# A table of some 3,500 steps, made anew: attention and a GELU MLP on one core

## The chip, the cores and the metric

One core of a Trainium2 chip runs the whole program. The metric is device time in microseconds (us), the median of several executions; smaller is better. TensorE (PE) multiplies matrices, VectorE (DVE), ScalarE (ACT) and GpSimd (POOL) work on tiles in SBUF and PSUM, and SyncE (SP) issues every DMA of this kernel. Each engine runs its own instructions strictly in the order in which the program gives them, and waits for the others through semaphores.

## What is computed

```python
scores = (q @ k^T) / sqrt(64)                 # 8 batches x 8 heads, 576 positions, 64 wide
scores = where(0 <= i-j < 128, scores - slope_h*|i-j|, -1e9)
x = softmax(scores) @ v                       # then as 4608 tokens x 512
h = x @ w_in                                  # 512 -> 2048
out = gelu(h) @ w_out                         # 2048 -> 512
```

All inputs and the output are fp32.

## The kernel before

**Tiles.** The 4,608 tokens are nine tiles of 512; a batch has 576 tokens, so batch b fills the end of tile b and the beginning of tile b+1. While the MLP of tile t runs, the attention of batch t+1 is made. A batch has four units, one for each pair of heads.

**Accuracy.** A factor is split into an fp16 high part and an fp16 low part, and a product is three fp16 products added in PSUM. So each operand that another engine makes costs a high part (a scaled copy) and a low part (a subtraction, mostly on DVE).

**One unit of attention** goes through these steps, named by a letter, the unit k and for M and N the half r of the unit's columns:

- S: scores on PE (L640). B: scale and bias from PSUM to SBUF on DVE (L666), with a memset on POOL (L672).
- M: softmax. A maximum on DVE (L749), exponentials on ACT (L753), the sums inverted on DVE (L756, L757), the weights scaled on POOL (L763, a piece of 128x192 each), the high part by a cast on ACT (L765).
- N: the low part of the weights, a subtraction on DVE (L772), and then a DMA on SP that transposes both parts into `et` (L776). A unit has two such halves, N{k}0 and N{k}1.
- Y: weights times v on PE (L821). It can start when the transposes have landed. X: the result as high and low part of x (ACT L841, DVE L323).

**One tile of the MLP.** In tiles 1 and 2 h is made by L868 (step H) and GELU follows (g). From tile 3 on h is made in blocks by sums of sub-blocks (steps 1 to 7, L1080 on PE; a, c, d, e with L1122 and L323 on DVE, L1131 on POOL), for which step Z makes sums of x first: `Z0` on POOL, `Z1` on DVE (L1004 to L1013). The second matrix is step o (L913; L910 in tile 0; one step of a tile is 12 matmuls). Tiles 7 and 8 have sub-block sums in the second product as well (L1230). The statistics of the next batch's v and q are the steps v and q: an absolute maximum over v (L391, DVE), then short operations that bring it over the partitions (L293 to L304, DVE), then powers of two and scales (L313 to L318, L522, L563).

**The order.** No scheduler decides it. Every step is a Python generator, and a long string names which one goes on next; the order of the steps is the order of the instructions on each engine. Two more strings tell which PSUM bank and which output buffer each allocation takes, in that order.

```python
    with tc.manual_schedule(engines=None):
        for step in ORDER.split():
            next(later[step])
```

In `ORDER`, a step's first digit is the tile in whose time it stands and the rest is as above: `3N31` is the second half of the low weights of unit 3 in the time of tile 3 (batch 4). A leading `0` before another digit is such a step that the tasks of the first tiles hold (`02y3`: batch 2, unit 3).

Of the kernel before, what the change touches and what calls it, by code (L numbers as in the profile page):

```python
# [68 lines left out]
0H2 0j6 0j5 0j3 0H5 0H5 0lv 0H0 0p2 0H1 0j4 0L2 0L3 0H5 0a6 0p2 0i4 0lv 0j5 0j5 0lv 0i4 0H4 0H5 0H8 0H9 0H9 0H9 0a7  # L69
0a7 0j3 0j3 0i5 0i5 0H8 0H8 0g1 0H11 0H11 0g4 0j7 0H9 0a6 0H11 0g3 0j6 0j6 0H10 0p3 0i3 0i3 0f 0p3 0A0 0p3 0p3 0p3  # L70
0H10 0H10 0j7 0j7 0g2 0H6 0H6 0lv 0v1 0i6 0H6 0i6 0g0 0H8 0i7 0H6 0H10 0i7 0p2 0f 0f 0A1 0p3 0J0 0H11 0A0 0A2 0J0 0J0
0lq 0lq 0f 0J2 0g11 0H7 0H7 0H7 0g5 0A2 0v1 0v1 0v1 0v1 0v1 0g9 0H15 0H15 0H15 0H15 0H7 0g7 01c 0v1 0v1 01c 0A1 0g8
0J2 0H12 0J2 0J1 0J1 0J1 0f 0u1 0q1 0q1 0u1 0q1 0q1 0H12 0q1 0q1 0q1 0A3 0J3 0A3 0J3 0J3 0H14 0H14 0H13 0H13 0H14 0H14
0H12 0H13 0O 0O 0q1 0d 0q1 0q1 0q1 0g6 0O 0O 0O 0H13 0g13 0g14 0O 0O 0d 0f 0A4 0f 0H12 0g15 0A4 0S1 0B1 0B1 0B1 0B1
0S0 0B0 0A5 0O 0B0 0B0 0g10 0S0 0S0 0B0 0B0 0B0 0S1 0S1 0B0 0B0 0B0 0g12 0M00 0o 0o 0J4 0J4 0J4 0M00 0B1 0B1 0J6 0o 0o
0o 0o 0A6 0J5 0M01 0M01 0M01 0M01 0M01 0S2 0M00 0A6 0M00 0J6 0J6 0f 0M01 0M01 0lV 0M10 0M00 0S2 0M00 0o 0o 0M01 0O
0M00 0M00 0M00 0A5 0M00 0M00 0M00 0M00 0N00 0N00 0N01 0N00 0N00 0N00 0A7 0M01 0lV 0M01 0M01 0J7 0B1 0lV 0B1 0N01 0N01
# [36 lines left out]
2H13 2H13 2M11 2g15 2g15 2g15 2B2 2M21 2M11 2M11 2o1 K K K K 2H14 2H13 2H13 2g13 2g13 2g14 2g14 2g13 K K 2M20 2g14 K
# [1348 lines left out]
```

## Time and profile before

| | us |
|---|---|
| median of 3 runs | 874.3 (873.79 to 874.45) |
| profiled execution | 870.3 |
| its span | 868.2, granted clock 0.998 |
| PE busy | 840.5 (97%) |
| DVE busy | 719.7 (83%) |
| ACT busy | 618.6 (71%) |
| POOL busy | 322.3 (37%) |

The profile was taken in one execution, 4.0 us below the median of the runs. A timeline row gives the start, the length, the engine, the line, the operation with the tiles it writes and reads, the number of instructions run together into the row, and in brackets how long the engine had stood idle before it and what released it. A view by windows gives each engine's busy time in a stretch and the granted TensorE clock there.

### The profile page before, as it was taken

Reading aid. Unit: us, or ns where it says so; the run is one execution under the profiler, and the core shown is the slowest. Engines: PE = TensorE matmul, PEld = TensorE weight load, DVE = VectorE, ACT = ScalarE, POOL = GpSimd, SP = SyncE. Lnnn points to the kernel's source line nnn. Section 1 sums busy time; section 2 is a strip of 40 time slices with the busy share of each in tenths; the row PEclk is TensorE's granted clock in tenths of the full one; section 3 lists DMA queues with packets and bytes.
Section 4 is the critical chain, followed back from the end, with each engine's and each line's share of the span. In section 5 each row is a group of like instructions: output and inputs, shape, how many; then the busy total and the mean of one; then the engine's idle time right before and its main releaser. Section 6 shows DMA issues by size and latency. Waiting matters only on the chain.

```text
span 868.2 us, 19703 instructions
## 1 busy us (share of the span) xinstructions
PE 840.5 (97%) x7860; PEld 548.4 (63%) x7860; DVE 719.7 (83%) x1278; ACT 618.6 (71%) x1246; POOL 322.3 (37%) x509
## 2 busy tenths in 40 slices
PE   6999999999999999999989998999999999999998
PEld 4654444544554455884568555865587467888887
DVE  6999999999899976988996989789868856774763
ACT  7999898887778867766758776765776646654661
POOL 2010100242027674577614973477526762000000
PEclk9999999999999999999999999999999999999999
DMA  9755485534553457474754685447651673341301
GB/s 314 272 165 200 157 246 148 145 108 112 111 140 123 107 172 208 139 160 137 166 155 157 143 206 176 141 86 194 177 196 16 182 181 146 121 159 31 117 1 49
DMA packets 180939, 129.45 MB, mean 149 GB/s; under 512 B 134384, under 2 KB 157040, under 8 KB 177136
## 3 DMA queue, kind: packets, MB, share of 16 engines
q1 hardware_dynamic: 180848, 128.21, 51.2%
q8 instruction: 61, 1.00, 0.5%
q14 instruction: 30, 0.25, 0.1%
HBM read 75.89 MB, written 17.83 MB: 108 GB/s over the span
## 4 chain that ended last, share of the span: by engine, by line
PE 47%; DVE 12%; POOL 4%; ACT 4%; DMA 3%; issue 2%; SPq 0%; DVEq 0%; POOLq 0%; ACTq 0%
PE u L1080 14%; PE v L1080 10%; PE o L913 7%; PE h L868 5%; PE u_out L1230 4%; POOL s L763 2%; DVE s L666 2%; PE sc L640 2%; DMA k<-kp 2%; PE av L821 1%; DMA et<-e_main 1%; DVE e_main L772 1%; PE z_out L1230 1%; PE x_out L1230 1%; PE v_out L1230 1%
## 5 line engine op out<-in xcount | busy, mean ns | idle before, releaser
L913 PEld LDWEIGHTS <-g 128*128 128x128 f16 x1152 | 111.1, 98 | 131.9 <-POOL g L891 0.6
L913 PE MATMUL o<-wo,g 128*128 128x512 f16 x864 | 191.8, 379 | 0.0
L753 ACT ACTIVATE s<-s,nmax 128x192 f32<-128x192 f32 x252 | 111.4, 443 | 32.3 <-DVE nmax L749 31.8
L868 PE MATMUL h<-x,wi 128*128 128x512 f16 x576 | 128.1, 379 | 0.3 <-DVE wi L323 0.2
L763 POOL TENSOR_SCALAR s<-s,z 128x192 f32<-128x192 f32 x180 | 103.1, 588 | 33.4 <-DVE z L757 20.0
L1080 PEld LDWEIGHTS <-t 128*128 128x128 f16 x1008 | 98.3, 98 | 12.2 <-DMA t<-stored 0.3
L868 PEld LDWEIGHTS <-wi 128*128 128x128 f16 x576 | 55.3, 98 | 68.9 <-issue 2.3
L1080 PEld LDWEIGHTS <-wi 128*128 128x128 f16 x864 | 84.3, 98 | 13.2 <-issue 1.4
L666 DVE SCALAR_TENSOR_TENSOR s<-sc,cs,bias_h 128x384 f32<-128x384 f32 x112 | 65.0, 605 | 1.9 <-PE sc L640 1.0
L913 PE MATMUL o<-wo_first,g 128*128 128x512 f16 x288 | 66.0, 379 | 0.1
L672 POOL MEMSET s<- 64x64 f32 (+1 forms) x112 | 19.2, 172 | 116.5 <-DVE s L666 103.3
L749 DVE TENSOR_REDUCE nmax<-s 128x5 f32<-128x960 f32 (+1 forms) x56 | 58.0, 1042 | 3.6 <-POOL s L672 2.6
L1080 PE MATMUL u<-xs,t 128*128 128x256 f16 x504 | 60.3, 273 | 0.0
L772 DVE TENSOR_TENSOR e_main<-s,e_main 128x768 f16<-128x768 f32 (+1 forms) x40 | 47.6, 1196 | 12.7 <-ACT e_main L765 12.7
L910 PE MATMUL o<-zo,g 128*128 128x512 f32 x128 | 56.9, 597 | 0.0
L640 PE MATMUL sc<-kbuf,qbuf 64*64 64x192 f16 (+3 forms) x1656 | 48.9, 251 | 7.6 <-ACT qbuf L541 4.4
L821 PE MATMUL av<-et,vbuf 128*64 128x64 f16 (+2 forms) x1392 | 43.4, 221 | 10.7 <-DMA et<-e_main 9.0
L1131 POOL TENSOR_SCALAR g<-rooms,sg 128x512 f16<-128x512 f32 x48 | 39.1, 820 | 36.5 <-issue 19.2
L821 PEld LDWEIGHTS <-vbuf 128*64 128x64 f16 x1392 | 40.7, 112 | 18.4 <-issue 14.8
L765 ACT CAST e_main<-s 128x768 f16<-128x768 f32 (+1 forms) x40 | 35.9, 905 | 21.7 <-POOL s L763 15.0
L323 DVE SCALAR_TENSOR_TENSOR g<-rooms,sg,g 128x512 f16<-128x512 f32 x48 | 41.8, 885 | 7.1 <-POOL g L1131 7.1
L753 ACT ACTIVATION_READ_ACCUMULATOR s<-s,nmax 128x1 f32 x252 | 47.3, 188 | 0.0
(253 smaller groups left out, 1697.2 us busy)
## 6 DMA issues: line engine op xcount, KB each, us to landing
t<-stored SPq DMA_DIRECT2D x21, 1024.0 KB, 5.2
v<-vp SPq DMA_DIRECT2D x32, 320.0 KB, 4.6
out<-ob SPq DMA_DIRECT2D x34, 256.0 KB, 2.7
raw<-w_in SPq DMA_DIRECT2D x8, 1024.0 KB, 10.8
raw<-w_out SPq DMA_DIRECT2D x8, 1024.0 KB, 6.3
q<-qp SPq DMA_DIRECT2D x7, 1152.0 KB, 5.7
k<-kp SPq DMA_DIRECT2D x7, 1152.0 KB, 7.0
stored<-sums SPq DMA_DIRECT2D x8, 512.0 KB, 2.6
```

The source lines that it names most:

```text
L640: done = nc.tensor.matmul(ps[bank][o, n, gap:W], a, m[:, gap:W], start=(i == 0 and (n == 0 or b > 0)), stop=(i == len(terms) - 1 and b > 0 ...
L666: yield nc.vector.scalar_tensor_tensor(out=s[:, bank[0] : bank[0] + k, :], in0=ps[bank][:, 0:k, 0:W], scalar=cs, in1=bias.broadcast_to([P, ...
L749: yield nc.vector.tensor_reduce(out=nmax[:, r], in_=s[:, r], axis=AX.X, op=ALU.max, negate=True)
L753: yield nc.scalar.activation(s[:, i, :], s[:, i, :], AF.Exp, bias=nmax[:, i : i + 1], accum_out=z[:, i : i + 1])
L763: yield nc.gpsimd.tensor_scalar(to, s[:, i], z[:, i : i + 1], 1.0, op0=ALU.mult, op1=ALU.mult)
L772: yield nc.vector.tensor_tensor(out=e[:, r, 1, c], in0=st.s[:, r], in1=e[:, r, 0, c], op=ALU.subtract)
L821: done = nc.tensor.matmul(av[r, (js[0] - blocks[0]) * QB : (js[-1] + 1 - blocks[0]) * QB], v32s[b][:, hp, kb, r] if b < EXACT else vbuf[:, ...
L868: done = nc.tensor.matmul(ph, wi[n][:, a, cc, k * P : (k + 1) * P], x[:, cc, b, :], start=(i == 0), stop=(i == 3 * NCC - 1),)
L910: done = nc.tensor.matmul(o, g[:, r, c], zo[n][:, n % 2, k * DM : (k + 1) * DM], start=(fc == first), stop=(fc == last))
L913: done = nc.tensor.matmul(o, g[:, r, a, c], wo[n][:, b, k, :], start=(fc == first and i == 0), stop=(fc == last and i == 2),)
L1080: done = nc.tensor.matmul(ps[:, k * HT : (k + 1) * HT], w(a, i)[:, k * P : (k + 1) * P], m(b, i), start=first and n == 0, stop=True, skip_ ...
L1230: done = nc.tensor.matmul(self.ps[name][:, tb], f(d, a)[:, k, tb * P : (tb + 1) * P], w(d, b, k), start=first, stop=True, skip_group_check ...
```

## The change

The string `ORDER` is another one from its tenth line on (the first 255 of its 3,534 steps, about 54 us, are the same), and with it `PSUM_BANKS` and `ROOMS`. The steps are the same ones, each as often as before; every engine has the same instructions with the same operands' sizes. The table is one line shorter, so every line of code behind it has a number lower by one after the change (L763 is L762). The line of the table in which the scores of unit 3 stand in the time of tile 3, and two lines of the other strings:

```diff
-3M20 3M20 L 3M20 3M20 3M11 3M21 3S3 3N11 3N11 3M21 3M21 3M21 3o1 3o1 3M20 3M20 3Q 3B3 3B3 3B3 3B3 3B3 3q 3M21 3v 3M21
+3M11 3o0 3M11 411 3B2 3B2 3B2 L 3c3 3o0 3B2 3e3 3M11 3v L L L 3M20 3k0 3k0 3o2 3N10 3M20 3S3 3N10 3v 3v 3v 3B2 3M21 L
...
-    "0123456701234567012345760215761340213402135017624762426734015327160725072450372450245450245061450741"
+    "0123456701234567012345760215761340213402135017624762426701325674250671307641307130713130713052106401"
...
-    "20120120202102102012102121201021212102102102120210210120210121210121120221021010120202120120"
+    "20121202002201210220210212120122220102101201201022102012012021012010210121021020202012012012"
```

On PE the scores of unit 3 in the time of tile 3 (`3S3`) stand 12 matmuls of the second matrix (one step o) earlier: between them and the first matmul of `3Y3` there were 96 of those and now there are 108, and that first matmul of `3Y3` is the same PE instruction, counted from the program's start, in both.

**POOL, in the time of tile 3, between unit 3's scores and `3Y3`** (`s_3` are the weights of unit 3, `xr_0` the sums of step Z0 for tile 4). Before:

```order
L1131 TENSOR_SCALAR g_3_4907<-m_3_2_4917,sg_0_3432 128x2x256
L763 TENSOR_SCALAR s_3_5377<-s_3_5377,z_3_5391 128x192 x9
L1004 TENSOR_TENSOR xr_0_5698<-x_4192 128x1024
L1006 TENSOR_TENSOR xr_0_5698<-xr_0_5698 128x256
L1007 TENSOR_TENSOR xr_0_5698<-xr_0_5698 128x256
```

Now:

```order
L1130 TENSOR_SCALAR g_3_4875<-m_3_2_4920,sg_0_2687 128x2x256
L762 TENSOR_SCALAR s_3_5387<-s_3_5387,z_3_5435 128x192 x5
L1003 TENSOR_TENSOR xr_0_5610<-x_4150 128x1024
L1005 TENSOR_TENSOR xr_0_5610<-xr_0_5610 128x256
L762 TENSOR_SCALAR s_3_5387<-s_3_5387,z_3_5435 128x192 x4
L1006 TENSOR_TENSOR xr_0_5610<-xr_0_5610 128x256
```

Two sums of step Z0 now stand ahead of the last four pieces of the unit's weights.

**DVE, in the time of tile 5, the second weights of unit 1** (`s6_1`; `stv7` is the statistic of the last batch's v). Before:

```order
L772 TENSOR_TENSOR e_main_95<-s6_1_7769,e_main_95 128x5x192
L756 TENSOR_SCALAR z6_2_8003<-z6_2_8003 128x5
L522 TENSOR_SCALAR cx6_6_8013<-pwv6_6525,sx6_6820 128x1
L772 TENSOR_TENSOR e_main_95<-s6_1_7769,e_main_95 128x4x192
L757 RECIPROCAL z6_2_8003<-z6_2_8003 128x5
L749 TENSOR_REDUCE nmax6_2_7934<-s6_2_7894 128x4
L391 TENSOR_REDUCE stv7_8040<-v32_7_7675 128x1
L293 COPY quarters_8118<-stv7_8040 32x1
```

Now:

```order
L390 TENSOR_REDUCE stv7_7991<-v32_7_7676 128x1
L986 TENSOR_TENSOR wsums2_0_7825<-wsums2_0_7825 128x1024
L755 TENSOR_SCALAR z6_1_7947<-z6_1_7947 128x4
L756 RECIPROCAL z6_1_7947<-z6_1_7947 128x4
L292 COPY quarters_8067<-stv7_7991 32x1 x2
L322 SCALAR_TENSOR_TENSOR g5_3_7661<-rooms5_2_7618,sg5_0_6068,g5_3_7661 128x2x256
L771 TENSOR_TENSOR e_main_95<-s6_1_7759,e_main_95 128x5x192
```

The maximum over v stood behind the unit's two halves of second weights and now stands ahead of both; the other half's L771 follows seven rows later, with the next steps of the statistic (two more L292, L293, L295) between.

## Rows read from the trace of the kernel before

**Rows 1.** By windows: PE, PEld, DVE, ACT, POOL busy, granted clock, DMA share, GB/s.

```profile
54.00:300.00 246.00, 243.06 (x1847) 118.27 (x1845) 233.42 (x447) 207.75 (x413) 63.62 (x102) 1.00 0.52 151
383.70:432.50 48.80, 48.80 (x460) 26.47 (x453) 44.66 (x91) 31.36 (x76) 35.56 (x61) 1.00 0.61 147
470.00:525.00 55.00, 55.00 (x560) 32.74 (x558) 50.31 (x101) 39.89 (x94) 41.43 (x69) 1.00 0.64 157
438.01:442.00 3.99, 3.99 (x51) 3.37 (x52) 3.31 (x6) 1.94 (x3) 0.25 (x1) 0.59 0.81 236
520.00:540.00 20.00, 16.87 (x243) 10.45 (x242) 17.97 (x34) 12.21 (x13) 7.13 (x7) 1.00 0.55 158
```

**Rows 2.** Timeline of PE: rows that PE came to after a wait.

```profile
152.46 1.58 PE L821 MATMUL av<-et,vbuf 128*64 128x256 f16 x54 [1.30 <-DMA et<-e_main]
...
244.83 2.34 PE L821 MATMUL av<-et,vbuf 128*64 128x256 f16 x72 [0.68 <-DMA et<-e_main]
...
353.08 2.78 PE L1080 MATMUL v<-x,wi 128*128 128x256 f16 x24 [0.68 <-DVE s L666]
...
438.01 2.17 PE L821 MATMUL av<-et,vbuf 128*64 128x256 f16 x42 [3.31 <-DMA et<-e_main]
...
532.28 1.59 PE L821 MATMUL av<-et,vbuf 128*64 128x128 f16 x60 [3.13 <-DMA et<-e_main]
...
596.40 2.72 PE L821 MATMUL av<-et,vbuf 128*64 128x128 f16 x78 [0.79 <-DVE s L666]
...
623.29 1.54 PE L821 MATMUL av<-et,vbuf 128*64 128x128 f16 x42 [0.58 <-DMA et<-e_main]
...
720.23 0.71 PE L1080 MATMUL u<-xs,qbuf 128*128 128x256 f16 x5 [1.43 <-ACT room_s L1187]
```

**Rows 3.** Timeline of DVE: rows at which DVE waited for PE.

```profile
383.70 0.69 DVE L1122 TENSOR_TENSOR m<-v,m 128x512 f32<-128x512 f32 x1 [0.85 <-PE v L1080]
...
459.66 0.69 DVE L1122 TENSOR_TENSOR rooms<-v,rooms 128x512 f32<-128x512 f32 x1 [2.91 <-PE v L1080]
```

**Rows 4.** DVE, operations that the change moves, and the weights' low parts.

```profile
420.86 0.20 DVE L302 STREAM_TRANSPOSE back<-spread 32x32 f32<-32x32 f32 x1
...
428.58 0.55 DVE L323 SCALAR_TENSOR_TENSOR x<-av,cx,x 128x320 f16<-128x320 f32 x1
...
429.46 3.09 DVE L772 TENSOR_TENSOR e_main<-s,e_main 128x960 f16<-128x960 f32 x2
...
592.84 2.80 DVE L391 TENSOR_REDUCE stv<-v 128x1 f32<-128x2560 f32 x1
```

**Rows 5.** SP and the whole run: transposes of the weights, issue, and landing after it.

```profile
410.93 2.06 SPq L776 DMA_TRANSPOSE et<-e_main  x1
...
592.02 1.61 SPq L776 DMA_TRANSPOSE et<-e_main  x1
...
DMA to landing us min/median/max: 3.6/4.1/8.4
```

**Rows 6.** PE: weights times v of units 0 and 1, in tile 3's time.

```profile
414.71 2.88 PE L821 MATMUL av<-et,vbuf 128*64 128x256 f16 x84
```

**Rows 7.** DVE and POOL at 713 us: sums of step Z beside each other.

```profile
713.27 0.42 DVE L1006 TENSOR_TENSOR xr<-xr 128x256 f32<-128x256 f32 x1
713.72 2.30 DVE L1007 TENSOR_TENSOR xr<-xr 128x256 f32<-128x256 f32 x1
...
713.62 2.12 POOL L1013 TENSOR_TENSOR xs<-xr,xs 128x1024 f16<-128x1024 f32 x1 [4.21 <-ACT xs L1012]
```

**Rows 8.** POOL: the last weights of unit 3 in tile 3, and step Z0.

```profile
423.20 2.43 POOL L763 TENSOR_SCALAR s<-s,z 128x192 f32<-128x192 f32 x6 [1.60 <-DVE z L757]
425.60 2.12 POOL L1004 TENSOR_TENSOR xr<-x 128x1024 f32<-128x1024 f16 x1
427.80 0.72 POOL L1006 TENSOR_TENSOR xr<-xr 128x256 f32<-128x256 f32 x1
```

**Rows 9.** The page's groups: count, busy us, mean ns, idle before and releaser: the cast.

```profile
L765 ACT CAST e_main<-s 128x768 f16<-128x768 f32 (+1 forms) x40 | 35.9, 905 | 21.7 <-POOL s L763 15.0
```

More of the change, by code (lines that the diff above doesn't have):

```diff
@@ L73 @@
[L73 to L77, printed above, removed]
@@ new lines @@
+0O 0g12 0q1 0q1 0q1 0q1 0A3 0J3 0q1 0g11 0H7 0A3 0J3 0J3 0f 0q1 0q1 0O 0O 0g7 0O 0lV 0q1 0A4 0J4 0S1 0A4 0B1 0S0 0B0
+0H14 0S0 0S0 0B1 0B1 0g14 0B0 0o 0lV 0B0 0B0 0B0 0B0 0A5 0B0 0B0 0J5 0M00 0M00 0M00 0o 0J4 0B0 0M01 0J6 0S1 0S1 0M00
+0o 0o 0J4 0f 0o 0A6 0B1 0B1 0B1 0B1 0M00 0M00 0M10 0A6 0S2 0M01 0M01 0S2 0o 0o 0o 0o 0B1 0o 0M01 0M01 0M00 0J6 0M00
+0M00 0M00 0M00 0lV 0M00 0M00 0B1 0M11 0M11 0M11 0M01 0N00 0N00 0J6 0N00 0N00 0N00 0M10 0M01 0M01 0M01 0M01 0A5 0N01
+0N01 0N01 0M10 0N00 0M01 0N01 0B2 0N01 0M10 0B2 0B2 0B2 0B2 0M20 0S3 0M10 0M10 0M10 0M11 0S2 0M11 0M11 0M10 0M10 0M10
@@ new lines @@
+0O 0J5 0J5 0O 0O 0M20 0M20 0O 0O 0A7 0B2 0M10 0M10 0B2 0M20 0M20 0M20 0B2 0lQ 0B2 0M21 0M11 0M11 0N10 0N10 0N10 0M20
+0lQ 0N11 0M11 0N11 0M10 0S3 0N10 0M21 0M11 0M11 0N10 0N11 0N11 0B3 0B3 0A7 0B3 0zs 0B3 0M21 0M21 0M21 0J7 0tl 0J7 0J7
+0M21 0zs 01c 0S3 0N11 0v2 0B3 0B3 0q2 0q2 0zs 0o 0O 0O 0O 0v2 0v2 0v2 0v2 0v2 0zs 0v2 0zs 0zs 0zs 0M21 0M21 0M21 0M21
+0o 0M21 0o 0Y0 0B3 0B3 0M30 0N10 0M20 0M20 0M20 0v2 0M30 0M20 0M20 0B3 0y0 0zs 0M20 0q2 0q2 0Y1 0M31 0M30 0M30 0M31
+0zs 0k3 0q2 0M30 0N21 0v1 0N21 0q2 0q2 0v2 0v2 0N20 0N20 0q2 0N20 0N20 0N20 0v2 0y1 0x1 0q2 0v2 0v2 0k2 0v2 0v2 0q2
@@ new lines @@
+03q 03q 0h2 0h2 01g1 02B1 02B1 01H2 01g1 01g4 02B1 01g2 01g2 01H10 01H10 01H10 02B1 0h2 01s 02S1 02S0 02B0 0h3 01H8
+01H8 01H6 02B0 02B0 01g2 01g1 01H10 01g10 02B0 01g10 02B1 02B1 02B1 01H5 02u 01H5 02M00 01H5 01H5 01g5 01H9 01H9 01H9
+01H14 01H14 01H14 01H6 01H6 02B1 01H14 01H12 01H12 02M01 01H12 01g5 02M10 01g5 0h3 02M00 02M00 02B1 02M11 0h3 0h3
+01H12 0h3 01g10 01H13 01g0 02u 03v 03v 0v2 02M01 02M01 02M01 02M01 01H13 01H13 01H15 02M00 02M00 02M00 02M00 01g12
+01H13 01g12 01H8 02M01 02M01 02M01 01H15 02M00 02M00 02M00 01g7 01g7 02M00 01H6 03Q 01g12 03Q 01H15 01H15 01o3 03v
@@ new lines @@
+2o3 2o3 2Y2 2X1 2Y2 2o3 2N30 2M31 2M31 2N31 2N31 2Y3 2Y3 3T1 2q 2q 2q 2q 2X2 2q 2q 2q 2q 2q 2q 2q 2q 2q 2Z0 2Z0 2q 2q
+2o3 2q 2q 2X2 310 2X0 2q 2q 2k2 2q 2q 2q 2Z0 2Z0 2Z0 2X3 2X3 2k3 2X2 2X2 3gs 2Z0 312 3S0 2X3 2X3 2Z1 3B0 2Z1 2Z1 2Z1
+3a0 311 321 3a1 3T0 3a2 3B0 3B0 3B0 2Z1 2Z1 3U 4gs 320 3B0 3B0 2Z1 323 3M00 3M00 3M00 361 3c1 3a1 3a0 3U 3M00 3M00
+3M00 360 3c0 3B0 2k2 3a0 3B0 3B0 371 3a1 350 370 3d0 3M00 3M00 3M00 3M00 3M00 3d1 3a1 3M00 3a1 351 3d1 3M00 3M00 3d0
+3d0 3d0 313 3a3 340 3e0 3a0 341 3N00 3e0 3M01 3a3 3T2 3d1 3d0 330 3e1 3e1 3e1 3d1 3M01 3M01 322 2k3 3T3 362 3c0 3e0
@@ L195 @@
+    "7364102357102365470236452364531264023615023615762035760215764207641203162403612703612407513407651234"
+    "70623470364512065432016541405716245037624056240752630460235412765024132673401536"
 )
 ROOMS = (
-    "20120120202102102012102121201021212102102102120210210120210121210121120221021010120202120120"
+    "20121202002201210220210212120122220102101201201022102012012021012010210121021020202012012012"
 )
```

216 lines of the change are left out of this document (99 added, 117 removed).

## The prediction

> **What bounds the kernel now.** The table shows PE busy for 840.5 of 868.2 us. The change gives PE the same instructions, so it can only move the 27.7 us in which PE stood idle, and the few in which its clock was low. Part of that idle time lies in the first 54 us, which do not change, and behind the last matmul, where both tables end with the same steps. So I read PE's waits first [rows 2]: between 54 and 865 us the longest have one cause. In five of these eight rows the product of weights and v waits for the transposed weights. The two longest, 3.31 and 3.13 us, belong to unit 3 in the time of tiles 3 and 4. Then the windows [rows 1]: behind the 3.31 us wait the granted clock was 0.59 for 3.99 us, that is a mean between the two levels, 1.2 and 2.4 GHz; behind the 3.13 us wait it stayed at 1.00. So the first wait cost 3.99 x 0.41 = 1.6 us more than itself.
>
> Next, who makes the weights late. DVE was busy for 233.4 of 246.0 us from 54 to 300 us, 44.7 of 48.8 us before the 3.31 us wait and 50.3 of 55.0 us before the other [rows 1]. It runs through its list almost without a gap there, and then, at 459.66, waits 2.91 us for PE [rows 3]. So in each tile DVE falls behind PE by the end of the attention and catches up in the middle products. Within such a stretch the delay of PE at a product with v is: where the weights' last operation stands on DVE's list, against where the product stands on PE's. **That is the measure I price the change by**: for each product, how many DVE operations came ahead of its weights, less how much PE work came ahead of it. A wait that stands earlier in the same stretch is not added to a later one; the later only takes what is missing.
>
> **The change, stretch by stretch.** *54 to 360 us.* At 152.46 the weights move ahead by 1.0 us on DVE and the product back by some matmuls, so the 1.30 us wait [rows 2] goes. The operations that made room stand a little later: 3.4 us more of short DVE operations now come before batch 2's unit 1, and the product of unit 0 and 1 there may wait up to 2 us. What PE gains or loses in this stretch it meets again at 353.08, where the first middle product waited 0.68 us [rows 2] for the end of DVE's work on unit 0 of the next batch; DVE's list up to there is the same within 0.5 us. I take **-0.2**; the ends are -2.7 (1.30 + 0.68 + 0.68, all these waits gone) and +1.5.
>
> *Tile 3.* PE reaches both products at the same place of its list as before. Ahead of unit 1's second weights there are now eight short operations of the statistic of v and the scales, 0.2 us or less each [rows 4], together 1.4 us. The transpose was issued at 410.93 and lands 4.1 us later by the median [rows 5], 415.0; unit 1's product is the second half of the row at 414.71 [rows 6], whose two units alternate, and needs it at 415.2. So there is 0.2 us to spare, and a new wait of 1.2 us. For unit 3, one low part of x of 0.55 us and one short operation went behind the weights [rows 4], three short ones ahead: 0.5 us earlier. The total delay at the product of unit 3 then is 3.3 - 0.5 = 2.8 us, of which 1.2 is already waited out at unit 1 and 1.6 stands at unit 3: **-0.5**. The earlier scores (the 108 matmuls instead of 96) do not add to this, because DVE's list and not the scores set the end; if they do, it is a gain, the third rival below. And no wait in this stretch is as long as 3.13 us, after which the clock stayed up: the fall goes, **-1.6**; the ends are -1.6 and 0.
>
> *The two sums of Z0 on POOL, now ahead of unit 3's last four pieces.* Before, POOL was through at 425.60 [rows 8], a cast takes 0.9 us [rows 9], and DVE took up the last low part only at about 429.46 + 1.55 = 431.0 [rows 4]: 4.5 us to spare. The sums cost 2.12 + 0.72 = 2.8 us [rows 8]. So they hide behind DVE's list, and I cost them at **0**; that cover is what the slower rival takes away.
>
> *Tile 4.* PE's places are again the same. A low part of x more (0.55), a short operation less ahead of unit 3's weights: **+0.4** on 3.13. Unit 1's weights come 1.3 us later, and what that makes PE wait is taken off the wait at unit 3.
>
> *Tile 5.* The maximum over v, 2.80 us [rows 4], and six short operations, some 0.9 together, now come ahead of unit 1's second weights: 3.7 us. The transpose was issued at 592.02 [rows 5] and lands at 596.1; the product is the last 42 of the 78 matmuls from 596.40 on [rows 2], that is from 597.7 on: 1.6 us to spare, so a new wait of 2.1 us. The 0.79 us wait at 596.40 stays. At 623.29 the 0.58 us wait goes: the product stands 2.7 us later on PE's list, its weights 0.6 us later on DVE's. 0.79 + 2.1 against 0.79 + 0.58: **+1.5**; the ends are 0 and +2.3 (no spare time beyond the issue's own length).
>
> *Into tile 7.* The first product with sums of x waited 1.43 us [rows 2]; 12 more middle matmuls, 0.116 us each by the row at 353.08 [rows 2], now stand between: **-1.4**. Two POOL sums of weights that ran beside DVE's sums of x here come earlier as well, which only makes this surer.
>
> Sum: -0.2 - 0.5 - 1.6 + 0.4 + 1.5 - 1.4 = **-1.8 us**. The profiled execution was 870.3 us, 4.0 below the median; 870.3 becomes 868.5, and the median 874.3 becomes **872.5 us**. The bound for faster or slower is 0.2%, 1.75 us: what a measurement of this kernel can tell from no change. The forecast lies on it.
>
> **Rivals.** *1. The clock falls all the same.* After the change the delay in tile 5 is 2.1 us in one wait and in tile 4 up to 2.5; a few tenths more and one of them is as long as the one that the clock fell after. For it: two waits on the edge. Against: one of 3.13 us left it up. Then the 1.6 us stay: -0.2, 874.1 us.
>
> *2. Slower: POOL's two sums are no longer hidden.* They read and write SBUF while DVE runs through short operations and low parts there. In the rows, a sum on DVE took 2.30 us while a sum ran on POOL for 2.12, against 0.42 for one of the same size just before [rows 7]: 1.9 us blocked. The Trainium skill (SBUF — State Buffer, Who interferes with whom) says that a DVE instruction with two SBUF inputs and a GpSimd instruction that reads SBUF contend for a shared pair of ports, a lock which whoever comes first holds for its whole instruction; the rows agree, and by that rule each two-input DVE operation can hold up each sum in its turn. As a mechanism here: from 425.60, 2.8 us of sums, one or two such blocks of 1.9 us, four pieces of 2.43/6 = 0.4 us [rows 8], so POOL ends at 431.9 or 433.8, the cast at 432.8 or 434.7, against the 431.0 at which DVE could have gone on: 1.8 to 3.7 us late. It decides from the point where POOL's last piece ends behind about 430. Unit 3's delay is then 3.3 + 1.8 = 5.1 us instead of 2.8, +2.3, and the clock falls, +1.6: -1.8 + 3.9 = +2.1, **876.4 us**, and 878.3 with the second block. For it: the sums wait for DVE's x, so the two engines meet just there. Against: there were 4.5 us to spare.
>
> *3. Much faster: DVE's list itself runs tighter.* DVE stood idle 4.1 us before the 3.31 us wait and 4.7 us before the other [rows 1], for ACT and POOL. With unit 3's scores earlier, part of it can be filled. If all of what is left at the two products goes (2.8 and 3.5 us), it is -1.8 - 6.3 = -8.1, 866.2 us; with half, 869.4. For it: the scores of unit 3 stand earlier in tiles 0, 2, 3, 4 and 5. Against: the operations ahead on DVE are nearly the same ones.
>
> **Chances.** Forecast 0.42 (its own range 870.5 to 874.0), rival 1 0.13, rival 2 0.24, rival 3 0.21. The forecast's 0.42 falls about evenly on both sides of the bound, which makes faster 0.44, same 0.32, slower 0.24. The range reaches from rival 3's end to rival 2's: 866.0 to 878.3.
>
> **What would show it.** In the changed profile: no wait at the product of unit 2 near 152 us; waits of about 1 us at unit 1 and under 2 us at unit 3 in tile 3's time, with a granted clock of 1.00 behind them; some 2 us in front of unit 1's product in tile 5's time, behind the maximum over v; none at the first product with sums in tile 7. Wrong it is if POOL's last piece of unit 3 releases the cast that DVE waits for, if the clock falls in another place, or if PE idles somewhere where it did not wait before, above all in tiles 6 and 7, where DVE's list moved by 1 to 3 us against PE's and I found the spare time to cover it.

## The result and the profile after

The changed kernel took **863.2 us** (median of four executions, 861.02 to 864.64) against 874.0 beside it: ratio **0.9878 [0.9852, 0.9904]**, 10.9 us less by the medians. Compared again beside later runs, it took 863.7 us, 0.9900 [0.9882, 0.9917]. The forecast of 872.5 and the whole range from 866.0 up are missed, on the faster side. The profiled execution after the change took 863.2 us, of which the span is 861.0.

The page's busy times after the change (share of the span, instructions):

```profile
PE 841.5 (98%) x7860; PEld 549.7 (64%) x7860; DVE 708.1 (82%) x1278; ACT 619.2 (72%) x1246; POOL 315.8 (37%) x509
```

Every count is the same as before, but DVE is busy 11.6 us less (719.7 before) and POOL 6.5 us less (322.3). The prediction had left no room for that.

Where PE stopped idling, by windows (stretch, its length, then PE, PEld, DVE, ACT and POOL busy, granted clock, DMA share, GB/s). First the kernel before, in stretches beside that of [rows 1]:

```profile
300.00:370.00 70.00, 67.91 (x712) 43.37 (x711) 53.92 (x93) 49.33 (x96) 40.11 (x54) 1.00 0.59 170
370.00:460.00 90.00, 86.67 (x873) 58.08 (x872) 78.17 (x138) 59.74 (x126) 48.77 (x81) 0.98 0.62 159
460.00:560.00 100.00, 96.87 (x1053) 67.80 (x1052) 86.61 (x150) 75.27 (x154) 58.94 (x100) 1.00 0.59 161
560.00:660.00 100.00, 98.23 (x992) 68.70 (x990) 82.11 (x146) 62.45 (x134) 55.70 (x87) 1.00 0.53 149
660.00:855.00 195.00, 193.37 (x1845) 153.95 (x1843) 136.01 (x209) 115.27 (x207) 45.35 (x68) 1.00 0.35 106
```

Then the changed kernel, cut at about the same work:

```profile
54.00:300.00 246.00, 246.00 (x1858) 119.50 (x1857) 232.48 (x453) 209.96 (x417) 54.74 (x102) 1.00 0.54 154
300.00:365.00 65.00, 64.21 (x695) 41.48 (x693) 49.19 (x89) 44.86 (x88) 36.40 (x52) 1.00 0.61 173
365.00:455.00 90.00, 89.98 (x919) 61.43 (x918) 79.20 (x143) 66.26 (x135) 57.55 (x87) 1.00 0.63 165
455.00:553.00 98.00, 94.90 (x1032) 65.85 (x1030) 84.90 (x148) 75.30 (x152) 58.60 (x92) 1.00 0.56 161
553.00:653.00 100.00, 98.94 (x1013) 69.28 (x1015) 82.63 (x147) 66.22 (x139) 57.85 (x91) 1.00 0.56 154
653.00:848.00 195.00, 192.71 (x1819) 152.94 (x1808) 132.52 (x208) 108.78 (x200) 41.69 (x64) 0.99 0.35 104
```

A stretch's length less PE's busy time is what PE stood idle:

| stretch, as before counts it | before | after |
|---|---|---|
| 54 to 300 us | 2.9 | 0.0 |
| 300 to 370 | 2.1 | 0.8 |
| 370 to 460 (tile 3) | 3.3 | 0.0 |
| 460 to 560 (tile 4) | 3.1 | 3.1 |
| 560 to 660 (tile 5) | 1.8 | 1.1 |
| 660 to 855 (into tile 7) | 1.6 | 2.3 |

With the start and the end it is 27.7 against 19.5 us, 8.3 less before rounding; 1.1 of it is given back as PE's busy time (841.5 less 840.5, before rounding): this execution had two falls of the clock and the one before had one. That makes the 7.2 us between the two spans.

The waits of PE behind 360 us, in the timeline of the changed kernel (the row of 429.15 had none):

```profile
429.15 3.10 PE L820 MATMUL av<-et,vbuf 128*64 128x256 f16 x84
...
502.18 1.59 PE L820 MATMUL av<-et,vbuf 128*64 128x128 f16 x60 [0.37 <-DMA et<-e_main]
...
523.67 1.59 PE L820 MATMUL av<-et,vbuf 128*64 128x128 f16 x60 [2.73 <-DMA et<-e_main]
...
588.93 1.54 PE L820 MATMUL av<-et,vbuf 128*64 128x128 f16 x42 [0.76 <-DVE back L301]
...
621.15 1.47 PE L1079 MATMUL v<-x,wi 128*128 128x256 f16 x12 [0.29 <-DVE s L665]
...
711.77 1.67 PE L1079 MATMUL u<-xs,qbuf 128*128 128x256 f16 x12 [2.29 <-ACT room_s L1186]
```

Against [rows 2]: tile 3's wait of 3.31 us is gone, tile 4's 3.13 us is split into 0.37 and 2.73, and the wait into tile 7 has grown from 1.43 to 2.29. In tile 5 the 0.79 us in unit 0's product and the 0.58 us are gone, a wait of 0.76 us stands ahead of unit 1's product, and one of 0.40 us for DVE's L666 (at 630.55, not in [rows 2]) is 0.29.

Why tile 3's wait is gone can be read to a few tenths. Before, DVE last waited for PE at 383.70 [rows 3], and PE came to unit 3's product at 438.01 - 3.31 = 434.70: 51.0 us of PE work. After the change the same DVE row begins at 379.69, and the product is the second half of the row at 429.15, at 430.7: again 51.0 us. DVE needed from there to the end of the last low weights 429.46 + 3.09 - 383.70 = 48.85 us before [rows 4], and 424.64 + 1.37 - 379.69 = **46.3** after, 2.5 us less. DVE's timeline in the changed kernel up to that end, and POOL's beside it:

```profile
418.67 1.74 DVE L299 COPY spread<-top 32x32 f32<-32x32 f32 x1
...
420.67 0.93 DVE L303 TENSOR_SCALAR stq<-back 32x2 f32<-32x2 f32 x3
422.07 1.32 DVE L771 TENSOR_TENSOR e_main<-s,e_main 128x960 f16<-128x960 f32 x1 [0.47 <-ACT e_main L764]
...
424.64 1.37 DVE L771 TENSOR_TENSOR e_main<-s,e_main 128x768 f16<-128x768 f32 x1
```

```profile
418.25 2.12 POOL L1003 TENSOR_TENSOR xr<-x 128x1024 f32<-128x1024 f16 x1 [2.19 <-DVE square L293]
420.45 0.72 POOL L1005 TENSOR_TENSOR xr<-xr 128x256 f32<-128x256 f32 x1
421.15 2.53 POOL L762 TENSOR_SCALAR s<-s,z 128x192 f32<-128x192 f32 x4
```

The two low parts take 1.32 + 1.37 = 2.69 us instead of 3.09 [rows 4], and the three L303 that lie together 0.93; in the kernel before, four of that operation took 2.99:

```profile
425.56 2.99 DVE L304 TENSOR_SCALAR stq<-back 32x2 f32<-32x2 f32 x4
```

DVE also stood idle 3.4 us in its stretch instead of 4.1 (46.3 less 42.9 busy; before by [rows 1]). So the 2.5 us come apart into 0.5 for operations that changed place (one low part of x and two short ones, as the prediction counted), 0.7 of idle time, and 1.3 of durations. The largest of these are the four L304 on `stq` (3.0 to 1.2), four low parts of the GELU (4.1 to 3.2) and the low weights (0.4); against them stand the copy (1.74, before 0.38) and some shorter ones. The rest of the wait is on SP. The answers on the lines that issue the transposes, unit 3's two each, the kernel before first:

```profile
L776 SPq DMA_TRANSPOSE et<-e_main x2: 2247/2316/2386, 431.2 to 433.6; - x2
...
DMA to landing us min/median/max: 4.2/4.6/5.1
```

```profile
L775 SPq DMA_TRANSPOSE et<-e_main x2: 1692/2102/2512, 423.5 to 426.0; - x2
...
DMA to landing us min/median/max: 4.1/4.3/4.5
```

Before, DVE was done at 432.55, but the first issue held SP for over 2 us, and the second began at 433.6 and landed 4.2 us later, at 437.8: 5.3 us behind DVE. After, the halves stand 2.5 us apart; the second is issued at 426.0, when DVE is done, and lands 4.5 us later, at 430.5. That saves another 0.8 us. 2.5 + 0.8 is the 3.31 us wait, and PE now comes to the product 0.2 us behind the landing, the same time that lay between landing and product before.

### The profile page after: what moved, and what is told of

The parts are those of the page before. It is cut to its first block, busy times and chain, and to the rows that moved or that the text cites. A ratio compares the mean times of both kernels' runs of the same rounds, so it can differ in the third digit from the quotient of the medians.

```text
span 861.0 us, 19687 instructions
## 1 busy us (share of the span) xinstructions
PE 841.5 (98%) x7860; PEld 549.7 (64%) x7860; DVE 708.1 (82%) x1278; ACT 619.2 (72%) x1246; POOL 315.8 (37%) x509
## 4 chain that ended last, share of the span: by engine, by line
PE 64%; DVE 9%; ACT 4%; DMA 4%; issue 2%; POOL 1%; SPq 1%; DVEq 0%; ACTq 0%; POOLq 0%
PE o L912 19%; PE u L1079 13%; PE v L1079 10%; PE h L867 9%; PE u_out L1229 4%; PE av L820 3%; PE sc L639 2%; DMA k<-kp 2%; DMA stored_out<-wsums 1%; PE z_out L1229 1%; PE y_out L1229 1%; PE x_out L1229 1%; PE v_out L1229 1%; DVE g L322 1%; DVE s L665 1%
## 5 line engine op out<-in xcount | busy, mean ns | idle before, releaser
L752 ACT ACTIVATE s<-s,nmax 128x192 f32<-128x192 f32 x252 | 111.3, 444 | 28.8 <-DVE nmax L748 27.3
L762 POOL TENSOR_SCALAR s<-s,z 128x192 f32<-128x192 f32 x180 | 100.6, 577 | 39.5 <-DVE z L756 31.5
L671 POOL MEMSET s<- 64x128 f32 (+1 forms) x112 | 19.2, 173 | 114.5 <-DVE s L665 103.7
L771 DVE TENSOR_TENSOR e_main<-s,e_main 128x960 f16<-128x960 f32 (+1 forms) x40 | 45.7, 1144 | 17.3 <-ACT e_main L764 17.2
L764 ACT CAST e_main<-s 128x960 f16<-128x960 f32 (+1 forms) x40 | 36.1, 906 | 23.6 <-POOL s L762 16.4
```

The costliest lines, as they stand in the source:

```text
L752: yield nc.scalar.activation(s[:, i, :], s[:, i, :], AF.Exp, bias=nmax[:, i : i + 1], accum_out=z[:, i : i + 1])
L762: yield nc.gpsimd.tensor_scalar(to, s[:, i], z[:, i : i + 1], 1.0, op0=ALU.mult, op1=ALU.mult)
```

## The experiments

A mixture of two tables goes from one order to the other between two tiles or steps (the seam); the strings of PSUM banks and buffers are joined to fit, and that matters, as the first three show. All runs compute the whole result. Ratios are to the kernel before on the same chip. Lines of the tables in the diffs are pieces, cut at both ends, without the bank digits that go with a moved step.

**The new order up to a seam, then the old one.** Three seams: at tile 3's first step, in the middle of tile 3, and in tile 5 before unit 3's softmax. The second and third were meant for the first middle products of tiles 4 and 6 and stand earlier, so what was expected of them holds for other seams than these.

```diff
 seam:  first step of tile 3 | middle of tile 3 | tile 5, unit 3's softmax
-before it: as before
+before it: as in the change
 behind it: as before
```

> The new table up to the first middle product of tile 3, from there the old order. Theory 1 (each tile stands alone, because DVE waits for PE at 383 us before): only the idle time before about 353 us goes, 1.3 + 0.7 + 0.7 + 0.5 us, so -3 us against before, with the wait at unit 3 in tile 3's time still 3.3 us. Theory 2 (a lag of DVE is carried from tile to tile): that wait falls below 1.5 us as well, with the low clock behind it: -6 or more. Theory 3 (the distance from scores to product decides): as theory 1.

> The new table up to the first middle product of tile 4, then the old order. Theory 1: the 3.3 us wait in tile 3's time and the low clock behind it go as well, so -8 us against before; the wait in tile 4's time stays 3.1 us. Theory 2: the wait in tile 4's time falls below 2 us too, -9 or more. Theory 3: as theory 1.

> The new table up to the first middle product of tile 6, then the old order. All theories: waits in tiles 4 and 5 as in the new kernel (0.4 + 2.7 and 0.8), so -9 us against before; the wait before tile 7's first product with sums stays 1.4 us or less, which the new kernel has at 2.3. If the last stretch of the new table is worth more than 1 us in either direction, this run shows it.

Measured: 883.8 us, 1.0136 [1.0116, 1.0156]; 884.9, 1.0150 [1.0129, 1.0171]; 869.6, 0.9976 [0.9963, 0.9988]. None answers the question, for behind the seam PE waits where neither table does. The first of them, PE's timeline:

```profile
512.35 2.77 PE L821 MATMUL av<-et,vbuf 128*64 128x128 f16 x60 [5.41 <-DVE x L323]
...
580.24 4.44 PE L913 MATMUL o<-wo_first,g 128*128 128x512 f16 x12 [2.98 <-POOL wsums L982]
```

A product of weights and v has no operand in x: by the releaser, what it waits for there is its PSUM bank, which the low part of x still reads. The next run bears this out.

**The same first seam with other banks, and its counterpart.** Between the first of these and the first one above only numbers in the two strings differ; the first line that does:

```diff
-    "7337413721537070125035647301472301472301406721067235067425374625104735647356207314560731546202736415"
+    "7337413721537070125035647301472301472301406721067235067425374625104735647356207314560731546275436201"
```

The counterpart is the old order up to tile 3's first steps and the new one from there.

```diff
 before the seam: as before
-behind it: as before
+behind it: as in the change
```

> As the first run (new table up to the first middle product of tile 3, from there the old order), but the PSUM banks behind the seam follow the old table's own succession, so that the seam adds no waits for a bank. Theory 1 (each tile stands alone): -3 to -4 us against before; the wait at unit 3 in tile 3's time stays between 2.4 and 3.4 us. Theory 2 (a lag of DVE is carried on): that wait is under 1.5 us and the time -6 us or better.

> The complement: the old order up to the first middle product of tile 3, from there the new table. Theory 1: the waits before 353 us stay (1.3, 0.6 and 0.9 us), the one at unit 3 in tile 3's time is gone: -5 to -7 us, and with the run before this one it adds up to the whole change. Theory 2: part of the waits in tiles 3 and 4 comes back (over 1.5 us more than in the new kernel), -3 us or less.

Measured: 868.4, **0.9956** [0.9941, 0.9971], and 865.9, **0.9926** [0.9904, 0.9948]. The banks alone had cost the first seam 15 us. In ratios the parts are -0.44% and -0.74%, together -1.18%, and the whole change was -1.22% and -1.00%: within their intervals they add up. With the new order up to tile 3 the early waits of [rows 2] are gone, and tiles 3 and 4 look as before:

```profile
432.96 1.59 PE L821 MATMUL av<-et,vbuf 128*64 128x256 f16 x42 [3.29 <-DMA et<-e_main]
...
527.26 2.76 PE L821 MATMUL av<-et,vbuf 128*64 128x128 f16 x60 [3.12 <-DMA et<-e_main]
```

With the old order up to tile 3, the waits at 152, 244 and 315 us stay (1.25, 0.85, 0.95) and unit 3's product in tile 3 has none. So each tile stands by itself, as the prediction had read from [rows 3], and an early gain does not go on into tile 3.

The two also show whose DVE durations they have. Groups by line on DVE, of the new order up to tile 3:

```profile
L323 DVE SCALAR_TENSOR_TENSOR g<-g,sg,g 128x512 f16<-128x512 f32 x32 | 24.5, 782 | 0.4 <-POOL g L891 0.3
...
L304 DVE TENSOR_SCALAR stq<-back 32x2 f32<-32x2 f32 x24 | 7.6, 316 | 0.4
```

and of the old order up to tile 3:

```profile
L322 DVE SCALAR_TENSOR_TENSOR g<-g,sg,g 128x512 f16<-128x512 f32 x32 | 27.3, 865 | 1.5 <-POOL g L890 1.2 <-ACT g L888 0.2
...
L303 DVE TENSOR_SCALAR stq<-back 32x2 f32<-32x2 f32 x24 | 4.3, 181 | 0.5
```

The first row, the low part of the GELU, belongs to tiles 1 and 2 only: it takes 24.5 us in all under the new order there and 27.3 under the old (24.3 and 27.3 in the two full tables). The second takes 7.6 us where the old order runs from tile 3 on and 4.3 where the new one does (4.4 and 7.6 in the full tables). **In these two groups a duration goes with the order around it**, and it is not a matter of the execution.

**The seam behind unit 3's products.** The new order up to unit 3's product in tile 3, and up to the one in tile 5.

```diff
 seam:  behind 3Y3 | behind 5Y3
-before it: as before
+before it: as in the change
 behind it: as before
```

> The new table through the product of unit 3 in the time of tile 3, then the old order. Theory 1: all waits up to there are the new kernel's (0.8 us in all behind 54 us), the wait at unit 3 in the time of tile 4 is 3.1 us as before, so -7 to -9 us against before. Theory 2: the wait in tile 4 falls under 2 us as well, -9 to -11.

> The new table through the product of unit 3 in the time of tile 5, then the old order. Waits up to there as in the new kernel, behind it 1.4 us or less before tile 7's first product with sums (the new kernel has 2.3). Theory 1 and 2 alike: as the new kernel or up to 1 us better, -10 to -12 against before. If the old order's end is worse than the new one's, it shows here as more than 1 us the other way.

Measured: 867.9, 0.9957 [0.9942, 0.9972], and 863.1, 0.9899 [0.9876, 0.9921]. The first adds nothing to the seam at tile 3, which missed what was expected of it: PE waits 1.18 us at unit 3's product and 2.81 us at tile 4's first product, for the low part of x. The second is as fast as the whole change, so what lies behind tile 5 brings nothing that these intervals show. In it the wait into tile 7 is 1.42 us, that of the old table.

**Unit 3's scores alone.** The old table, with the scores of unit 3 one step o earlier in tiles 3 and 4.

```diff
-3M11 3M11 3M11 3o2 3M11 3M11 3M21 3M11
-3M20 3M20 L 3M20 3M20 3M11 3M21 3S3 3N11
+3M11 3M11 3M11 3S3 3o2 3M11 3M11 3M21 3M11
+3M20 3M20 L 3M20 3M20 3M11 3M21 3N11
...
-4o1 4o1 4o1 L 4o1 4M10 4S3 4e3
+4o1 4o1 4o1 L 4S3 4o1 4M10 4e3
```

> The old table with one edit in two places: the scores of unit 3 in the time of tiles 3 and 4 stand one step o (12 matmuls, 2.6 us) earlier on PE, nothing else moves on any engine. Theories 1 and 2 (DVE's list sets the pace): the waits stay 3.3 and 3.1 us within 0.5, the time within 1 us of before. Theory 3 (the distance from scores to product decides): both waits shrink by 2.6 us to about 0.6, the clock stays up: -6.5 us.

Measured: 871.8, 0.9998 [0.9983, 1.0013], with waits of 3.38 and 3.22 us. While DVE's list stays the old one, the place of the scores on PE is worth nothing, as the prediction had it. Whether DVE could fill idle time by taking earlier scores up earlier, the reason that the third rival gave, was not tested: DVE's list is the same here.

**The changed kernel again,** beside the next runs.

> The new kernel itself once more, as the base for the runs beside it: ratio to the kernel before 0.988 (0.985 to 0.990), waits as in its first profile (0.8, 0.4, 2.7, 0.8, 0.3 and 2.3 us behind 54 us).

Measured: 863.7, 0.9900 [0.9882, 0.9917]. Its waits are those of the first profile: 2.69 us in tile 4, 0.69 in tile 5, 1.98 into tile 7.

**The low weights of unit 3 first.** In the old table's tile 3 and in the new table's tile 4, unit 3's low weights and transposes moved ahead of the end of q's statistic.

```diff
-3X0 3q 3q 3q 3q 3N21 3Y2 3Y2 3M31 3Z0 3X0 3q 3q 3N30 3N30 3N31 3N31 3Y3 3Y3
+3X0 3N21 3N30 3N30 3M31 3N31 3N31 3q 3q 3q 3q 3Y2 3Y2 3Z0 3X0 3q 3q 3Y3 3Y3
...
-4M30 4q 4q 4X1 4q 4q 4X1 4X0 4Z0 4Z0 4Z0 4M31 4N31 4Z0 4Z0 4N30 4q 4q 4Y2 4q 4N31 4N30
+4M30 4N30 4N30 4q 4q 4X1 4M31 4N31 4N31 4q 4q 4X1 4X0 4Z0 4Z0 4Z0 4Z0 4Z0 4q 4q 4Y2 4q
```

> The old table with one edit, in the time of tile 3: the low parts of unit 3's weights (two operations on DVE) and their transposes stand ahead of the last steps of the statistic of q on DVE, not behind them; nothing moves on PE or POOL. Theory A (order: the cast was ready at 426.3 and 427.4 us, DVE got to the low parts at 429.5 and 431.1): they end about 3 us earlier, the 3.3 us wait falls under 0.5, the clock stays up, -4 to -5 us. Theory B (amount: the list is as long as before, so what is not waited for here is waited for next): the wait comes back as one of 2 us or more at the first products of tile 4, which need x, or at the next scores, which need q: -1 us or nothing.

> The new table with the same edit in the time of tile 4: unit 3's low weights and their transposes right behind their casts (511.4 and 512.6 us in the new kernel; DVE got to them at 516.2 and 517.6), ahead of the end of q's statistic. Theory A: the 2.7 us wait goes, -2.7 us against the new kernel, and up to 1.6 more in those executions in which the clock fell behind it. Theory B: it comes back at the first products of tile 5, 0 to -1.

Measured: 873.3, 1.0012 [0.9999, 1.0026], and 862.4, 0.9896 [0.9877, 0.9915]. PE's timeline of the first:

```profile
435.90 1.54 PE L821 MATMUL av<-et,vbuf 128*64 128x256 f16 x42 [0.59 <-DMA et<-e_main]
...
441.07 2.72 PE L1080 MATMUL u<-x,wi 128*128 128x256 f16 x12 [3.63 <-DVE x L323]
```

The wait did go, from 3.31 to 0.59 us, and came back as 3.63 at the next product that hangs on DVE. The same run's ACT and DVE show how:

```profile
433.23 2.22 ACT L568 ACTIVATE qbuf<-q,scq 128x2304 f16<-128x2304 f32 x1 [5.22 <-DVE scq L318]
```

```profile
435.48 2.62 DVE L323 SCALAR_TENSOR_TENSOR qbuf<-q,scq,qbuf 128x2304 f16<-128x2304 f32 x1 [2.17 <-ACT qbuf L568]
```

The end of q's statistic, now behind the weights, gives the scale `scq` that ACT needs for the high part of q. DVE needs that high part for the low part of q, and reaches x only behind it: on that way it stood idle for 2.17 us. In the second run, 2.7 us became mainly 1.07 and, at the middle products behind, 1.61. **An operation moved ahead moved the wait and did not shorten it, because what it passed is waited for too.** The amount of DVE's time, as theory B had it, is only a part of the reason: the first run's DVE had a gap.

**A store ahead of a load.** In the changed kernel SP issues a load of 1 MB just before the store of weight sums that frees `xs`.

```diff
-6N30 6N30 7T0 6o3 6X1 6X1 L
+6N30 6N30 6o3 6X1 6X1 L 7T0
```

> The new table with one DMA moved: the load of 1 MB for tile 7 (issued at 698.4 us) behind the store of the sums of weights (699.1, landed at 707.8), not ahead of it. The store's buffer is the next one of the sums of x: ACT waited for its landing 7.2 us. If that is the cause of the 2.3 us wait ahead of tile 7's first product with sums, the store lands by 702, the wait falls under 0.5 us, and the time is 2 to 3.5 us under the new kernel's. If the transposes beside it hold the store up, or the load then comes too late (needed at 715.8), the wait stays or moves: within 0.5 us.

Measured: 862.3, 0.9885 [0.9866, 0.9905]. The changed kernel's ACT and SP around that store:

```profile
707.85 1.99 ACT L1011 CAST xs<-xr 128x1024 f16<-128x1024 f32 x2 [7.20 <-DMA stored_out<-wsums]
```

```profile
698.44 0.57 SPq L994 DMA_DIRECT2D qbuf<-stored  x1
699.06 0.44 SPq L987 DMA_DIRECT2D stored_out<-wsums  x1
```

and PE with the two turned round:

```profile
711.26 1.47 PE L1079 MATMUL u<-xs,qbuf 128*128 128x256 f16 x12 [0.31 <-ACT room_s L1186]
```

The wait falls from 2.29 and 1.98 us in the two executions of the changed kernel to 0.31, so the load ahead of the store is shown to be its cause. The time is lower than the changed kernel's beside it by 1.5 us; their ratios overlap, and in the execution with the profile tile 4's wait was 3.27 us, so it can't be called faster.

**Which engine's order takes tile 3's wait away.** The new table with all of tile 3's stretch in the old order; with only PE's part of it old; with only PE's part new.

```diff
 tile 3's stretch, rest as in the change
-PE new, DVE ACT POOL SP new
+PE old, DVE ACT POOL SP old
+PE old, DVE ACT POOL SP new
+PE new, DVE ACT POOL SP old
```

> The new table, but from the first middle product of tile 3 to the product of unit 3 in its time in the old order, on all engines. Expected: the 3.3 us wait is back at that product, and the clock falls behind it: 3.3 to 5 us over the new kernel. If the seam behind it adds a wait for x, it is that much more.

> The new table; in the same stretch only PE runs in the old order, DVE, ACT, POOL and SP in the new one. Theory A (the lists of the other engines removed the wait): no wait over 0.7 us at unit 3's product, within 1 us of the new kernel. Theory B (PE's order did, by feeding DVE earlier): 2 to 3.3 us of wait there, 2 to 5 us over the new kernel.

> The complement: the new table; in the same stretch PE runs in the new order and DVE, ACT, POOL and SP in the old one. Theory A: the 3.3 us wait is there as in f1 (2.5 to 3.5). Theory B: under 1 us.

Measured: 869.0, 0.9975 [0.9960, 0.9990]; 876.5, 1.0074 [1.0055, 1.0092]; 866.4, 0.9955 [0.9939, 0.9970]. The first gives back 6.5 us against the second comparison of the changed kernel (0.9975 less 0.9900, 0.75% of 871.1): 2.99 us at unit 3's product, 0.48 and 0.78 at the seam, 3.29 for 2.7 in tile 4, and falls of the clock with both long waits. The second has no wait at unit 3's product, but up to 2.98 us in seven others earlier in tile 3, since PE's old order does not match the new lists. These add up to 10.7 us by which PE came later to everything behind, so that the missing wait proves nothing. The third, with PE's new order and the other engines' old lists, has the old wait back. Its timelines of PE and DVE:

```profile
434.87 2.77 PE L820 MATMUL av<-et,vbuf 128*64 128x256 f16 x42 [3.38 <-DMA et<-e_main]
```

```profile
422.39 2.98 DVE L303 TENSOR_SCALAR stq<-back 32x2 f32<-32x2 f32 x4
...
426.28 3.09 DVE L771 TENSOR_TENSOR e_main<-s,e_main 128x960 f16<-128x960 f32 x2
```

PE's order is the new one in this run and in the changed kernel, and only the lists of the other engines differ: they take the wait away, and PE's order alone does not. Whether the new lists would do so with PE's old order stays open. With the old lists the old durations are back too: 2.98 and 3.09.

**Is it POOL that makes them long?** The old table, with nothing changed in its order on PE; the five sums of `Z0` for tile 4 and the subtraction behind them (L1013) move from POOL to DVE, behind the low weights.

```diff
-nc.gpsimd if i == 0 and t < FAST else nc.vector
+nc.gpsimd if i == 0 and t < FAST and t != 4 else nc.vector
...
-3Y2 3Y2 3M31 3Z0 3X0 3q 3q 3N30 3N30 3N31 3N31 3Y3
+3Y2 3Y2 3M31 3X0 3q 3q 3N30 3N30 3N31 3N31 3Z0 3Y3
```

> The old table, but the sums of x for tile 4 that POOL made beside DVE's last operations of unit 3 are made by DVE instead, behind the unit's low weights. Theory C (DVE loses time beside POOL): the four short operations of q's statistic fall from 2.99 us to about 0.6 and the two low weights from 3.09 to 2.0 to 2.4, so the 3.3 us wait falls under 0.7; the sums then cost DVE some 3.8 us later, and a wait of 1 to 3 us appears at tile 4's first products. Theory D (POOL does not matter to DVE here): the same lengths and the same 3.3 us wait.

Measured: 870.3, 0.9988 [0.9975, 1.0002]. DVE's timeline, then PE's:

```profile
426.69 0.67 DVE L304 TENSOR_SCALAR stq<-back 32x2 f32<-32x2 f32 x4
...
428.58 2.03 DVE L772 TENSOR_TENSOR e_main<-s,e_main 128x960 f16<-128x960 f32 x2
```

```profile
436.65 1.54 PE L821 MATMUL av<-et,vbuf 128*64 128x256 f16 x42 [0.79 <-DMA et<-e_main]
...
446.14 1.47 PE L1080 MATMUL u<-x,wi 128*128 128x256 f16 x12 [1.24 <-DVE s L666]
```

With POOL's sums away, the same two groups take 0.67 instead of 2.99 us and 2.03 instead of 3.09: **3.4 us of DVE's time were POOL's doing in this one place**. The wait shrinks from 3.31 to 0.79. The run is hardly faster, if at all: DVE now makes the sums itself, and PE waits 1.24 us at tile 4's first products. In the changed kernel no run takes POOL's operations away.

## Why the prediction was wrong, point by point

**What bounds the kernel: right.** PE's idle time and the clock were all there was to win, and each tile stands by itself (the two runs with a seam at tile 3). In tile 3 the lists of the other engines set the wait (the run with PE's new order alone); into tile 7 it was SP's.

**The step that failed: "where the weights' last operation stands on DVE's list, against where the product stands on PE's".** I counted the operations that changed place, and took a place on the list for a time: every other operation kept its old duration, and DVE's idle time and the way from DVE to the landing stayed as they were. At unit 3 in tile 3 the places brought the 0.5 us that I gave them; the other 2.8 of the 3.3 us are durations (1.3), idle time (0.7) and the spacing of the two transposes (0.8).

The durations: over the program the same 1,278 instructions took 11.6 us less. As the last run shows for one place, a duration of DVE depends on what POOL does at that moment, and a new order makes new pairs. The prediction had such a pair in hand, 2.30 against 0.42 us [rows 7], yet used it for the slower rival alone, as something that the change could add. It did not ask how much of it the old order already contained: the 2.99 us for four operations of 32x2 elements stood in DVE's timeline between two rows that were quoted [rows 4]. One of the four is in the chain of work that ended last, on the way to the 3.31 us wait:

```profile
425.71 2.03 DVE stq L304
...
433.65 4.22 DMA et<-e_main
438.01 2.17 PE av L821 x34
```

The Trainium skill (SBUF — State Buffer, Who interferes with whom) says that a `tensor_scalar` or a copy, too, can take the ports that DVE shares with GpSimd, when its operands meet the conditions of a 2-port mode, and that whoever holds them makes the other wait for a whole instruction. The rows agree: the 2.03 us end at 427.74, and POOL's sum of 2.12 us [rows 8] ends at 425.60 + 2.12 = 427.72. The last run agrees too: 2.99 less 0.67 is 2.3 us for the group.

**54 to 360 us: -0.2 foreseen, -3.8 measured** by the new order up to tile 3 (0.44% of 871.7, by its interval 2.5 to 5.1 us), mostly beyond the end of -2.7. All waits of these stretches but one went (0.79 us at 311.88, before 0.86 at 315.87, which [rows 2] left out), 4.2 us of idle time in the two profiles. I had 3.4 us of short operations ahead of batch 2's unit 1 take back what the 1.30 us gave. The GELU's low parts there take 3.0 us less and POOL's scaling beside them 19.1 less 12.0 = 7.1. How the 3.8 us divide between such durations and the changed places stays open.

**Tile 3: -0.5 and -1.6 foreseen, -3.3 and -1.6 in the profiles.** The clock's fall went with the wait, as foreseen there. The new waits of 1.2 us at unit 1 and 1.6 at unit 3 did not come. At unit 1 the short operations did come ahead, 1.2 us of them, but DVE was through its weights 25.1 us behind the row of [rows 3] and not 27.2: its idle time up to there fell from 2.9 to 1.1 us, and other durations by 1.5.

**POOL's two sums ahead of the last pieces: cost 0, right, but narrowly.** ACT's casts of unit 3's weights in the changed kernel:

```profile
421.05 0.99 ACT L764 CAST e_main<-s 128x960 f16<-128x960 f32 x1 [2.95 <-DMA et<-e_main]
423.72 0.83 ACT L764 CAST e_main<-s 128x768 f16<-128x768 f32 x1 [1.68 <-POOL s L762]
```

The second waits for POOL's last pieces and ends at 424.55, and DVE takes up its low part at 424.64: 0.1 us to spare. DVE's wait of 0.47 us at 422.07 is for the first, which had waited for a transpose of the unit before to land and not for POOL. The slower rival's 1.9 us block did appear (1.74 us for a copy at 418.67, beside a POOL sum of 2.12), on an operation for which DVE had the time.

**Tile 4: +0.4 foreseen, 0.0 measured** (3.13 before, 0.37 + 2.73 after). **Tile 5: +1.5 foreseen, -0.7 in the profiles:** PE waits 0.76 us and not 0.79 + 2.1. The maximum over v fell into a gap. From the last L1122 on `m` (572.05 before, 563.44 after) to the end of unit 1's weights DVE needed 19.9 us both times: it is busy 19.7 and not 17.3 us there, and idle 0.2 and not 2.7. The 0.76 us came with the transpose, which took 5.4 us from issue to landing and not 3.8; why stays open.

**Into tile 7: -1.4 foreseen, +0.6 to +0.9 measured** (1.98 and 2.29 against 1.43; in the five other runs that have the new order there and the load ahead, 1.41 to 2.24). I counted twelve more matmuls as cover and left out SP: the store that frees the buffer of `xs` stands behind a load of 1 MB there. This was the only term with the wrong sign that cost time.

**The clock.** I took from one execution that it stays up behind a wait of 3.13 us. With the new order up to tile 3 the same wait (3.12) went with a granted clock of 0.50 from 526.5 to 527.2, while PE still stood idle, and of 0.77 in the 4 us from 528.0, and with the old order up to tile 3 one of 2.75 us with 0.74. Falls differ between executions of one program. In 86 executions of the kernel before, beside the runs above, the mean granted clock was 0.998 in 21 (median 870.2 us), 0.996 in 42 (871.7), 0.994 in 13 (873.5) and 0.992 in 10 (874.1). A step of 0.002 is 1.7 us, about one fall. The profile of before was taken in an execution at 0.998; that fits the medians' lying 10.9 us apart at first and the two profiles only 7.1. At 0.998 the changed kernel's five executions have a median of 863.1, again 7.1 below. The rest, 1.6 of the 8.7 us by which it was ahead in the second comparison (1.00% of 871.9; 8.1 by the medians), goes with fewer falls.

**The rivals.** The third named the right direction, "DVE's list itself runs tighter", and a part of the reason: idle time of DVE was filled (2.9 to 1.1 us and 4.1 to 3.4 in tile 3, 2.7 to 0.2 in tile 5). The operations that filled it in tile 5 are the statistic's; that earlier scores did is not shown, and the shorter durations it did not name. The second met its mechanism with the sign turned round.

**Open.** Which of the moves of DVE, POOL, ACT and SP in tile 3 counts how much was not separated; the runs tell PE's order from the others' only. Nor was the part of the new banks and buffers told from that of the order. No version was clearly faster than the changed kernel.

## What to carry to other kernels

Before pricing a reordering by places on a list, look on a saturated DVE for groups whose duration is far above that of the same operation elsewhere, and at what POOL runs beside them: that time is what a new order can win or lose. Before moving a waited-for operation ahead, look at who waits for what it passes. Do not take a list for gapless: work that falls into a gap costs nothing. Take the base from several executions' clocks, and follow each moved step on the DMA queue too.

## What the runs showed of the hardware that was not expected

Operations of a few elements can take as long as a large sum on POOL: 2.99 us for four `tensor_scalar` of 32x2 in one place and 0.67 in another, 1.74 us for a copy of 32x32 that took 0.38 in the kernel before. With the same lists these durations come back to a hundredth in some places (2.99 and 3.09 in the kernel before and with the new order up to tile 3, 2.98 and 3.09 with another PE order) and to a few tenths in others (0.66 and 0.37 us for one L312 in tile 3, in two executions of the changed kernel). And the clock's falls are no property of a wait's length alone: behind 3.13 us none in one execution, behind 2.29 and 2.75 us one each, and in the first 40 us, which no table changed, a granted clock of 0.71 from 32 to 36 us in one execution and 1.00 in another.
